# Rebuilding 64-bit weights as 32-bit numbers: two VectorE passes and two ScalarE passes in place of three and one

## The chip, the core and the metric

The kernel runs on one core of a Trainium2 chip. Its engines work side by side, each through its own queue in order: TensorE (PE, with its weight loads as PEld), VectorE (DVE), ScalarE (ACT), GpSimd (POOL) and SyncE (SP), which here issues DMA transfers. The metric is the device time of one execution, in microseconds. Three runs of the kernel before gave 382.01, 382.57 and 385.27 us; the median is 382.57 us.

## The reference

Three stages follow one another on inputs of 2 batches, 8 heads, 768 positions and 48 numbers per head.

```
state = 0
for t in range(768):                      # attention with a decay, per batch and head
    cur = outer(u * k[t], v[t])
    y[t] = r[t] @ (state + cur)
    state = w[t][:, None] * state + outer(k[t], v[t])
# first feed-forward block, x = y with heads side by side (384 wide)
xk = mu_k * x + (1 - mu_k) * x_prev ;  xr = mu_r * x + (1 - mu_r) * x_prev
k = relu(xk @ w_k) ;  v = (k * k) @ w_v ;  x = sigmoid(xr @ w_r) * v
# second block
h = gelu(x @ w_in) ;  u, v = halves of h
v_n = layer_norm(v) * g_ln ;  v_s = w_sg @ v_n + b_sg
out = x + (u * v_s) @ w_out
```

Five weight matrices (`w_k`, `w_v`, `w_r`, `w_in`, `w_out`) arrive as 64-bit floating-point numbers. The engines compute with 32 bits, so each is turned into 32-bit numbers on the chip.

## The kernel before, in words

**Units.** The attention is cut into groups of 384 positions (three chunks of 128; four groups) and pairs of heads (four), which makes 16 units, counted here from 1. For a unit, DVE makes running products of the decay (`pf`, `pr`) and scaled inputs (`rp`, `kp`; some on POOL), PE makes scores `sc`, DVE masks them (`am`), PE makes chunk states `kv`, ACT scales them (`pk`), DVE chains them (`us`, `ucar`), PE forms `y`, and DVE adds POOL's diagonal part `av` and writes `yt`. `av` comes from the unit's transfer `un`, multiplied twice on POOL (lines 360 and 361), summed on ACT (line 367) and multiplied again on POOL (line 372). PE then transposes `yt` to `xx`.

**Feed-forward steps.** For each group, `xx` is mixed with its neighbour position (`dx`, line 511), and multiplied by the weights (line 492). For most groups each operand is split in a high part (`...h`, a copy by ACT) and the rest (`...l`, a difference on DVE or POOL), and three products are added. For the first group the 32-bit weights `wk` and `wv` are used whole, and split afterwards: ACT copies `wkh`, `wvh` (line 241), POOL takes the difference `wkl`, `wvl` (line 242).

**Weights.** The 31 pieces of 128 x 384 weights (8 `wk`, 3 `wr`, 8 `wv`, 12 `wf`, the last for the second block) are converted by `load64` (lines 223 to 237). SP loads a piece as pairs of 32-bit words into a staging tile `stg`, of which there are three. ACT scales the high word by 2 to the power -112, which moves the exponent (line 233). DVE shifts left by 3 and clears the top bit (line 235), puts in the sign of the high word (line 236), and puts in the top three bits of the low word (line 237). The staging tile is free after line 237. The target tile of a `wf` piece comes from a ring of 24 tiles (tag `wl`), in which the first `wf` takes the place of a `wv` tile that POOL's line 242 reads.

**Order.** PE's order is written by hand, as a list of steps with planned times (`plan`). For the other engines each instruction gets a due time (`with at(...)`), and a scheduler at build time orders each engine's queue by due time and by its own estimate of when an instruction could start. SP and ACT also issue DMA transfers from their queues: SP the units' `ut` and the weights, ACT the units' `uv` and `un` (lines 211 and 213), so an instruction that waits at the head of such a queue also holds the transfers behind it.

Of the kernel before, what the change touches and what calls it, by code (L numbers as in the profile page):

```python
# [8 lines left out]
AF = mybir.ActivationFunctionType  # L9
ALU = mybir.AluOpType  # L10
# [47 lines left out]
def emit(tc, tin, nin, vt, consts, ubc, mu_k, mu_r, g_ln, b_sg, w_k, w_v, w_r, w_in, w_sgT, w_out, outT):  # L58
    nc = tc.nc
    V, A, PL, PE, SP = nc.vector, nc.scalar, nc.gpsimd, nc.tensor, nc.sync  # L60
# [162 lines left out]
    def load64(full, src, c0, c1, f0, f1, dl):  # L223
        n, f = c1 - c0, f1 - f0
        stg = pl["s"].tile([128, n, f, 2], U32, name="stg", tag="stg", bufs=B_STG)
        with at(dl - 7):
            SP.dma_start(
                stg.rearrange("p c f w -> p c (f w)"),
                src.bitcast(U32).rearrange("(c p) f -> p c f", p=128)[:, c0:c1, 2 * f0:2 * f1])
        wl, wh = stg[:, :, :, 0], stg[:, :, :, 1]  # L230
        bits = full.bitcast(U32)
        with at(dl - L_CV - 1):
            A.activation(full, wh.bitcast(F32), AF.Copy, scale=2.0 ** -112)
        with at(dl - L_CV):
            V.tensor_scalar(bits, bits, 3, 0x7FFFFFFF, ALU.logical_shift_left, ALU.bitwise_and)  # L235
            V.scalar_tensor_tensor(bits, wh, 0x80000000, bits, ALU.bitwise_and, ALU.bitwise_or)  # L236
            V.scalar_tensor_tensor(bits, wl, 29, bits, ALU.logical_shift_right, ALU.bitwise_or)  # L237

    def split_to(hi, lo, full, dl, e):
        with at(dl):  # L240
# [16 lines left out]
    def conv_moe1():  # L257
        def one(nm, i, src, box, dl):
            full1(nm, i, [128, KM, 128] if nm != "v" else [128, 1, DM])
            load64(wt[nm, i][0], src, *box, dl)  # L260
            if NAT[nm] == 0 or (nm == "v" and i >= NVN):
                split1(nm, i, dl - (3 if nm == "v" else 0))

        for f in range(KF):
            one("k", f, w_k, (0, KM, f * 128, f * 128 + 128), TS["k", 0, f])
        for f in range(KM):
            one("r", f, w_r, (0, KM, f * 128, f * 128 + 128), TS["r", 0, f])
        for f in range(KF):
            one("v", f, w_v, (f, f + 1, 0, DM), TS["v", 0, 0] + MM[0, "v"] * f)

    def conv_moe2():
        sp = split_ops[0]

        def make(key, shape):
            if sp:
                wt[key] = tuple(pl["b"].tile(shape, F32R, name="w2" + q, tag=f"w2{key[0]}{q}{key[1]}", bufs=1) for q in "hl")
            else:
                wt[key] = (pl["b"].tile(shape, F32, name="w2f", tag=f"w2{key[0]}f{key[1]}", bufs=1),)

        def fill(dst, src, box, dl):  # L280
            if sp:
                full = pl["w"].tile(list(dst[0].shape), F32, name="wf", tag="wl", bufs=NW1 + SPARE)
                load64(full, src, *box, dl)
                split_to(dst[0], dst[1], full, dl, PL)
            else:
                load64(dst[0], src, *box, dl)

        make(("in", "v"), [128, KM, DH])
        for x in range(KH):
            fill(part(wt["in", "v"], slice(None), slice(None), slice(x * 128, x * 128 + 128)), w_in,  # L290
                 (0, KM, DH + x * 128, DH + x * 128 + 128), TS["iv", 0, 0] - 6 + x)
        for x in range(KH):
            make(("in", x), [128, KM, 128])
            fill(wt["in", x], w_in, (0, KM, x * 128, x * 128 + 128), TS["iv", 0, 0] - 2 + x)
        for x in range(KH):
            make(("out", x), [128, 1, DM])
            fill(wt["out", x], w_out, (x, x + 1, 0, DM), TS["o", 0, 0] - 4 + x)
# [584 lines left out]
```

## Time and profile before

| | |
|---|---|
| runs | 382.01, 382.57, 385.27 us |
| profiled execution, first to last instruction | 380.1 us |
| busy: PE, PEld, DVE, ACT, POOL | 352.7, 317.3, 275.2, 183.6, 131.6 us |
| mean granted TensorE clock | 0.917 |

The profiled execution's own time is the span of 380.1 us; the median of the runs stands 2.5 us above it. All times inside the program are counted from the start of that span. A timeline row gives start, length, engine, line, operation and, in brackets, the idle time of the engine just before it and what ended it. PE counts as busy while a matmul is in its pipeline.

### The profile page before, as it was taken

Reading aid. Unit: us, or ns where it says so; the run is one execution under the profiler, and the core shown is the slowest. Engines: PE = TensorE matmul, PEld = TensorE weight load, DVE = VectorE, ACT = ScalarE, POOL = GpSimd, SP = SyncE. Lnnn points to the kernel's source line nnn. Section 1 sums busy time; section 2 is a strip of 40 time slices with the busy share of each in tenths; the row PEclk is TensorE's granted clock in tenths of the full one; section 3 lists DMA queues with packets and bytes.
Section 4 is the critical chain, followed back from the end, with each engine's and each line's share of the span. In section 5 each row is a group of like instructions: output and inputs, shape, how many; then the busy total and the mean of one; then the engine's idle time right before and its main releaser. Section 6 shows DMA issues by size and latency. Waiting matters only on the chain.

```text
span 380.1 us, 5744 instructions
## 1 busy us (share of the span) xinstructions
PE 352.7 (93%) x1971; PEld 317.3 (83%) x1971; DVE 275.2 (72%) x561; ACT 183.6 (48%) x542; POOL 131.6 (35%) x185
## 2 busy tenths in 40 slices
PE   5999898988897699899999999999999999999993
PEld 1889676657657598799989999989999998999993
DVE  6789988999977989963564997229898971735531
ACT  1354646866828576243565849456834323501100
POOL 0657974561699967541301653000000000000000
PEclk9555657989899699999999999999999999999999
DMA  7975357556641363400001130091233001010011
GB/s 176 273 238 177 98 186 222 152 160 211 206 127 31 111 187 101 128 5 2 0 2 42 43 113 13 0 280 26 63 84 80 10 3 62 2 62 0 2 65 69
DMA packets 27125, 36.20 MB, mean 95 GB/s; under 512 B 3312, under 2 KB 21584, under 8 KB 27088
## 3 DMA queue, kind: packets, MB, share of 16 engines
q1 hardware_dynamic: 23056, 29.57, 25.7%
q10 hardware_dynamic: 4032, 6.19, 5.4%
q8 instruction: 17, 0.28, 0.3%
q14 instruction: 20, 0.16, 0.1%
HBM read 33.39 MB, written 2.36 MB: 94 GB/s over the span
## 4 chain that ended last, share of the span: by engine, by line
PE 49%; DVE 10%; ACT 5%; issue 3%; POOL 3%; ACTq 0%; POOLq 0%
PE mm L492 22%; PE mn L492 22%; PE y L456 2%; DVE dx L511 2%; DVE wf L236 2%; DVE wf L237 1%; DVE kl L548 1%; POOL av L361 1%; PE sc L394 1%; ACT wvh L241 1%; ACT kr L547 1%; ACT kr L533 1%; ACT kh L546 1%; DVE xrl L515 1%; DVE wf L235 1%
## 5 line engine op out<-in xcount | busy, mean ns | idle before, releaser
L372 POOL TENSOR_TENSOR av<-uv,ac 128x96 f32<-128x96 f32 x48 | 30.5, 653 | 7.8 <-issue 4.4
L596 POOL TENSOR_SCALAR mv<-mv 128x1 f32<-128x1 f32 x12 | 2.9, 246 | 86.1 <-ACT vg L595 86.1
L456 PEld LDWEIGHTS y<-uv,am 128*128 128x128 f32 x192 | 29.2, 228 | 1.2 <-issue 0.6
L480 ACT ACTIVATE gah<-gt 128x384 fp32r<-128x384 f32 x16 | 8.4, 526 | 44.4 <-DVE gt L638 44.4
L533 ACT ACTIVATE kr<-mm 128x384 f32<-128x384 f32 x27 | 13.1, 485 | 30.9 <-PE mm L492 30.8
L456 PE MATMUL y<-uv,am 128*128 128x48 f32 x192 | 27.8, 303 | 0.0
L242 POOL TENSOR_TENSOR w2l<-wf,w2h 128x384 fp32r<-128x384 f32 x12 | 15.4, 1294 | 35.3 <-ACT w2h L241 35.0
L492 PE MATMUL mm<-xkh,wk 128*128 128x384 f32 x48 | 22.1, 609 | 0.0
L511 DVE SCALAR_TENSOR_TENSOR dx<-xx,par,dx 128x384 f32<-128x384 f32 x21 | 15.7, 760 | 8.4 <-ACT dx L508 8.3
L342 DVE TENSOR_TENSOR_SCAN pr<-ut,d1r 112x387 f32<-112x387 f32 x16 | 21.4, 1334 | 0.3
L367 ACT ACTIVATE av<-av 128x48 f32<-128x48 f32 x72 | 16.6, 245 | 10.0 <-POOL av L361 10.0
L394 PE MATMUL sc<-rp,kp 48*128 48x128 f32 x192 | 20.1, 352 | 1.3 <-DVE am L398 1.3
L492 PE MATMUL mm<-xkh,wkh 128*128 128x384 f32 x57 | 21.3, 373 | 0.0
L548 DVE TENSOR_TENSOR kl<-kr,kh 128x384 fp32r<-128x384 f32 x24 | 17.9, 747 | 4.2 <-ACT kr L547 4.0
L398 DVE TENSOR_TENSOR am<-sc,cst 128x384 f32<-128x384 f32 x32 | 17.0, 544 | 4.7 <-PE sc L394 4.7
L394 PEld LDWEIGHTS sc<-rp,kp 48*128 48x128 f32 x192 | 16.3, 243 | 4.7 <-issue 1.8
L492 PE MATMUL mn<-wsh,vh 128*128 128x384 f32 x60 | 20.1, 334 | 0.0
L492 PE MATMUL mn<-wsh,vl 128*128 128x384 f32 x60 | 20.1, 334 | 0.0
L492 PE MATMUL mn<-wsl,vh 128*128 128x384 f32 x60 | 20.1, 334 | 0.0
L492 PE MATMUL mm<-xkh,wkl 128*128 128x384 f32 x57 | 19.7, 346 | 0.0
L492 PE MATMUL mm<-xkl,wkh 128*128 128x384 f32 x57 | 19.7, 345 | 0.0
L338 DVE TENSOR_TENSOR_SCAN pf<-ut,d1f 112x387 f32<-112x387 f32 x16 | 15.6, 977 | 3.3 <-DMA ut<-tin 3.3
(209 smaller groups left out, 1153.2 us busy)
## 6 DMA issues: line engine op xcount, KB each, us to landing
ut<-tin SPq DMA_DIRECT2D x14, 505.8 KB, 4.2
un<-nin ACTq DMA_DIRECT2D x14, 288.0 KB, 3.8
stg<-w_k SPq DMA_DIRECT2D x8, 384.0 KB, 4.5
stg<-w_v SPq DMA_DIRECT2D x8, 384.0 KB, 3.6
stg<-w_in SPq DMA_DIRECT2D x8, 384.0 KB, 3.0
wq<-tin SPq DMA_DIRECT2D x16, 168.0 KB, 2.4
wsf<-w_sgT SPq DMA_DIRECT2D x12, 192.0 KB, 4.2
outT<-ot SPq DMA_DIRECT2D x12, 192.0 KB, 1.9
```

The costliest lines, as they stand in the source:

```text
L242: e.tensor_tensor(lo, full, hi.bitcast(F32), ALU.subtract)
L338: V.tensor_tensor_scan(pf[:, 0:n1], w[:, 0:n1], d1f[:, 0:n1], 1.0, ALU.mult, ALU.add)
L342: V.tensor_tensor_scan(pr[:, 1:wl][:, ::-1], w[:, 1:wl][:, ::-1], dr[:, 1:wl][:, ::-1], 0.0, ALU.mult, ALU.add)
L367: A.activation(z, z, AF.Copy, accum_out=ac[:, c, h:h + 1])
L372: PL.tensor_tensor(av[:, c].rearrange("p (h d) -> p h d", d=D), uv[i][:, c].rearrange("p (h d) -> p h d", d=D), ac[:, c, :, None].to_broad ...
L394: PE.matmul(sc[h][:, c], s["kp"][hs, c], s["rp"][hs, c], start=True, stop=True)
L398: V.tensor_tensor(am[:, h], sc[h], mask, ALU.mult)
L456: PE.matmul(o, l, r, start=(j == 0), stop=(j == len(mms) - 1), skip_group_check=True)
L492: PE.matmul(ps, l, r, start=(k == 0), stop=(k == len(prods) - 1))
L511: V.scalar_tensor_tensor(o, x[:, j, t0:t1], nu[:, j:j + 1], d, ALU.mult, ALU.add)
L533: A.activation(kr, ps, AF.Relu)
L548: V.tensor_tensor(kl, kr, kh.bitcast(F32), ALU.subtract)
```

## The change

`load64` gets a second ACT instruction and loses one of DVE's three. ACT reads the top byte of the low word (a byte in every eight), computes (byte + 0.5) / 32 - 0.5 and writes it, turned into a whole number, over the low word: that is the byte's three top bits. DVE then shifts the scaled high word left by 3 and puts in these bits in one pass, and puts in the sign in a second.

```
         with at(dl - L_CV - 1):
             A.activation(full, wh.bitcast(F32), AF.Copy, scale=2.0 ** -112)
+            top = stg.rearrange("p c f w -> p c (f w)").bitcast(mybir.dt.uint8).rearrange("p c (f w) -> p c f w", w=8)[:, :, :, 3]
+            A.activation(wl, top, AF.Copy, bias=0.5 / 32 - 0.5, scale=1.0 / 32)
         with at(dl - L_CV):
-            V.tensor_scalar(bits, bits, 3, 0x7FFFFFFF, ALU.logical_shift_left, ALU.bitwise_and)
+            V.scalar_tensor_tensor(bits, bits, 3, wl, ALU.logical_shift_left, ALU.bitwise_or)
             V.scalar_tensor_tensor(bits, wh, 0x80000000, bits, ALU.bitwise_and, ALU.bitwise_or)
-            V.scalar_tensor_tensor(bits, wl, 29, bits, ALU.logical_shift_right, ALU.bitwise_or)
```

In the changed kernel the second ACT instruction is line 235, the two DVE passes are lines 237 and 238, and all later lines count one more than before. PE's order is the same in both. The queues of ACT, DVE, POOL and SP are ordered anew at three places that the prediction speaks of.

First, ACT's queue where it issues the transfer of unit 10 (`un_980`). Before:

```order
L241 ACTIVATE wkh_779<-wk_115 128x384
L514 ACTIVATE xkh_1151<-dx_1158 128x384
L211 DMA uv_978<-nin 128x288
L559 ACTIVATE rs_1065<-mm_1055 128x384
L419 ACTIVATE pk_1071<-kv_1068,pb_867 112x48 x4
L233 ACTIVATE wv_239<-stg_240 128x384
L559 ACTIVATE rs_1088<-mm_1078 128x384
L213 DMA un_980<-nin 128x576
```

And now (`un_855` is the transfer of unit 9, which before stood further ahead):

```order
L560 ACTIVATE rs_1088<-mm_1078 128x384
L213 DMA un_855<-nin 128x576
L509 ACTIVATE dx_1153<-xx1_78,par_75 128x384
L509 ACTIVATE dx_1158<-xx1_78,par_75 128x384
...
L515 ACTIVATE xkh_1151<-dx_1153 128x384
L233 ACTIVATE wv_239<-stg_240 128x384
L235 ACTIVATE stg_240<-stg_240 128x384
L515 ACTIVATE xkh_1151<-dx_1158 128x384
L242 ACTIVATE wkh_779<-wk_115 128x384
L211 DMA uv_978<-nin 128x288
L213 DMA un_980<-nin 128x576
```

The steps on `dx` and `xkh` stood ahead of the transfer in both, but they now stand behind `rs_1088`; in DVE's queue the two `dx` now stand behind the `yt` of unit 8.

```order
L437 SCALAR_TENSOR_TENSOR us_1067<-ucar_81,pt_868,pk_1071 112x96
L237 SCALAR_TENSOR_TENSOR wv_218<-wv_218,stg_219 128x384
L437 SCALAR_TENSOR_TENSOR us_1067<-us_1067,pt_868,pk_1071 112x96
L238 SCALAR_TENSOR_TENSOR wv_218<-stg_219,wv_218 128x384
L460 TENSOR_TENSOR yt_726<-y_1090,av_871 128x3x96
L512 SCALAR_TENSOR_TENSOR dx_1153<-xx1_78,par1_76,dx_1153 128x384
L512 SCALAR_TENSOR_TENSOR dx_1158<-xx1_78,par1_76,dx_1158 128x384
```

That is DVE's queue of the changed kernel at the end of unit 8: the chain `us`, then `yt`, then the two `dx`.

Second, ACT's queue ahead of `pk_1286`, which unit 9's `y` needs. Before:

```order
L533 ACTIVATE kr_1240<-mm_1230 128x384
L386 ACTIVATE kt_1268<-kt_ps_1264 128x336
L546 ACTIVATE kh_1242<-kr_1240 128x384
L233 ACTIVATE wf_2299<-stg_2300 128x384
L547 ACTIVATE kr_1240<-kr_1240 128x384
L419 ACTIVATE pk_1286<-kv_1282,pb_992 112x48 x6
```

And now:

```order
L233 ACTIVATE wf_2299<-stg_2300 128x384
L235 ACTIVATE stg_2300<-stg_2300 128x384
L534 ACTIVATE kr_1240<-mm_1230 128x384
L387 ACTIVATE kt_1268<-kt_ps_1264 128x336
L547 ACTIVATE kh_1242<-kr_1240 128x384
L233 ACTIVATE wf_2308<-stg_2309 128x384
L548 ACTIVATE kr_1240<-kr_1240 128x384
L235 ACTIVATE stg_2309<-stg_2309 128x384
L420 ACTIVATE pk_1286<-kv_1282,pb_992 112x48 x6
```

The first `wf` has moved ahead of three steps, and a second `wf` with its extra step has come ahead of `pk_1286`.

Third, DVE's queue ahead of `us_1281`, the chain of unit 9. Before:

```order
L398 TENSOR_TENSOR am_1270<-sc_1272,cst_70 128x384
L235 TENSOR_SCALAR wf_2299<-wf_2299 128x384
L548 TENSOR_TENSOR kl_1243<-kr_1240,kh_1242 128x384
L236 SCALAR_TENSOR_TENSOR wf_2299<-stg_2300,wf_2299 128x384
L436 SCALAR_TENSOR_TENSOR us_1281<-pk_1286,pt_993 112x96
```

And now:

```order
L237 SCALAR_TENSOR_TENSOR wf_2299<-wf_2299,stg_2300 128x384
L238 SCALAR_TENSOR_TENSOR wf_2299<-stg_2300,wf_2299 128x384
L399 TENSOR_TENSOR am_1270<-sc_1271,cst_70 128x384
L399 TENSOR_TENSOR am_1270<-sc_1272,cst_70 128x384
L549 TENSOR_TENSOR kl_1243<-kr_1240,kh_1242 128x384
L237 SCALAR_TENSOR_TENSOR wf_2308<-wf_2308,stg_2309 128x384
L437 SCALAR_TENSOR_TENSOR us_1281<-pk_1286,pt_993 112x96
```

Both passes of the first `wf` and the first pass of the second now stand ahead of `us_1281`, and the two `am` behind the first `wf`. In POOL's queue one of the differences `wkl` has moved ahead of unit 10's `un` (lines 360 and 361); the rest of that stretch has the same instructions as before.

## Rows read from the trace of the kernel before

**Rows 1.** PE's waits by what ended them, from 40 to 110 us (ahead of the dots) and from 110 to 160 us (behind them): us in total, times, longest.

```profile
PE y L456 <- DVE us L436: 3.5, 5, 1.3
PE sc L394 <- DVE am L398: 1.3, 1, 1.3
PE mm L468 <- DVE yt L459: 1.0, 1, 1.0
PE mm L492 <- DVE wv L237: 1.0, 1, 1.0
...
PE y L456 <- DVE us L436: 3.7, 3, 2.9
PE y L456 <- ACT pk L419: 2.9, 1, 2.9
PE y L456 <- DVE pk L421: 1.6, 1, 1.6
PE kt_ps L468 <- DVE yt L459: 0.2, 1, 0.2
```

**Rows 2.** PE's waits from 160 us to the end.

```profile
PE kt_ps L468 <- DVE yt L459: 0.6, 1, 0.6
PE mn L492 <- DVE kl L548: 0.2, 1, 0.2
```

**Rows 3.** Stretches cut where the granted clock changes: stretch, then length, busy us (x instructions) of PE, PEld, DVE, ACT, POOL, then the granted clock, the DMA share and GB/s.

```profile
43.80:57.50 13.70, 13.00 (x51) 10.00 (x51) 12.18 (x24) 6.49 (x28) 11.32 (x14) 0.50 0.42 133
...
60.90:64.30 3.40, 3.40 (x6) 1.72 (x6) 2.69 (x7) 1.51 (x6) 1.46 (x3) 0.50 0.66 205
64.30:81.40 17.10, 15.48 (x87) 11.14 (x86) 16.71 (x33) 14.23 (x50) 9.59 (x14) 1.00 0.60 176
81.40:84.80 3.40, 3.40 (x9) 2.01 (x8) 3.40 (x7) 1.30 (x4) 2.40 (x3) 0.50 0.35 106
...
98.40:125.70 27.30, 22.57 (x101) 15.24 (x99) 22.04 (x31) 18.53 (x71) 26.87 (x28) 1.00 0.33 101
125.70:132.60 6.90, 4.91 (x20) 4.54 (x22) 6.87 (x9) 2.72 (x7) 6.41 (x8) 0.51 0.37 116
```

**Rows 4.** The pass that the change removes, and the near instructions for what it adds: groups by line with shapes; busy us, mean ns of one, then the idle time before them.

```profile
L235 DVE TENSOR_SCALAR wf<-wf 128x384 uint32<-128x384 uint32 x12 | 5.3, 446 | 2.0 <-ACT wf L233 2.0
L235 DVE TENSOR_SCALAR wk<-wk 128x384 uint32<-128x384 uint32 x8 | 3.8, 484 | 0.0
L235 DVE TENSOR_SCALAR wv<-wv 128x384 uint32<-128x384 uint32 x8 | 3.0, 370 | 1.1 <-ACT wv L233 1.1
L235 DVE TENSOR_SCALAR wr<-wr 128x384 uint32<-128x384 uint32 x3 | 1.7, 560 | 1.1 <-ACT wr L233 1.1
...
L236 DVE SCALAR_TENSOR_TENSOR wk<-stg,wk 128x384 uint32<-128x384 uint32 x8 | 4.9, 621 | 0.0
...
L233 ACT ACTIVATE wk<-stg 128x384 f32<-128x384 f32 x8 | 4.5, 564 | 0.0
...
L533 ACT ACTIVATE kr<-mm 128x384 f32<-128x384 f32 x27 | 13.1, 485 | 30.9 <-PE mm L492 30.8
L508 ACT ACTIVATE dx<-xx,par 128x384 f32<-128x384 f32 x24 | 13.9, 610 | 0.8 <-DVE xrl L515 0.7
L511 DVE SCALAR_TENSOR_TENSOR dx<-xx,par,dx 128x384 f32<-128x384 f32 x21 | 15.7, 760 | 8.4 <-ACT dx L508 8.3
```

**Rows 5.** The chain that ended last, in order of time, around unit 9's `y`: start us, us, what.

```profile
121.95 1.01 POOL wvl L242
...
122.98 0.56 ACT wf L233
...
125.39 1.27 DVE wf L236
126.66 0.98 DVE us L436
...
127.69 0.74 PE y L456 x2
```

**Rows 6.** POOL's timeline ahead of that.

```profile
98.75 0.83 POOL L360 TENSOR_TENSOR av<-un,u_sb 128x288 f32<-128x288 f32 x1 [2.85 <-DMA un<-nin]
...
100.41 2.59 POOL L242 TENSOR_TENSOR wkl<-wk,wkh 128x384 fp32r<-128x384 f32 x2
...
118.41 9.11 POOL L242 TENSOR_TENSOR wvl<-wv,wvh 128x384 fp32r<-128x384 f32 x8
```

**Rows 7.** The issue of unit 10's `un` on ACT (second row) with the step that held ACT (first row), and the last matmul of unit 8's `y`.

```profile
93.22 0.55 ACT L233 ACTIVATE wv<-stg 128x384 f32<-128x384 f32 x1 [1.25 <-DMA stg<-w_v]
93.22 0.33 ACTq L213 DMA_DIRECT2D un<-nin  x1
...
94.44 0.46 PE L456 MATMUL y<-us,rp 112*128 112x96 f32 x2 [0.83 <-DVE us L436]
```

**Rows 8.** From issue to landing of the transfers `un` (first) and `stg` (second).

```profile
DMA to landing us min/median/max: 2.5/4.1/5.8
...
DMA to landing us min/median/max: 2.7/3.6/7.1
```

**Rows 9.** ACT and DVE just ahead of unit 9's `y`.

```profile
121.40 0.47 ACT L533 ACTIVATE kr<-mm 128x384 f32<-128x384 f32 x1
...
123.85 0.28 ACT L419 ACTIVATE pk<-kv,pb 112x48 f32<-112x48 f32 x1
...
120.56 1.00 DVE L398 TENSOR_TENSOR am<-sc,cst 128x384 f32<-128x384 f32 x2
```

**Rows 10.** DVE's removed pass where it ran within POOL's stretch from 98.75 to 122.96 us, and POOL's difference in that stretch (times one: minimum, median, maximum ns).

```profile
99.27 0.53 DVE L235 TENSOR_SCALAR wv<-wv 128x384 uint32<-128x384 uint32 x1 [0.35 <-ACT wv L233]
...
L242 POOL TENSOR_TENSOR wvl<-wv,wvh x8: 998/1212/1343, 118.4 to 126.2; 128x384 fp32r<-128x384 f32 x8
```

## The prediction

> **What bounds the kernel now.** I began with PE's waits, because PE is busy for 352.7 of the 380.1 us. From 160 us to the end it waits 0.8 us in all [rows 2], though 12 of the 31 pieces of weights are partly converted there: nothing can be won in that half, and little lost while PE stays fed. From 40 to 110 us it waits 6.8 us, each time for DVE (3.5 for `us`, 1.3 for `am`, 1.0 for `yt`, 1.0 for a `wv`), and from 110 to 160 us 8.4 us [rows 1]. Two single waits of 2.9 us make most of the latter; both belong to unit 9's `y`. Next the stretches by granted clock: after several of these waits PE is granted 0.50, its lower level of 1.2 GHz, for 3.4 us at a time, and 6.9 us after the two long ones [rows 3]. DVE is busy nearly without a break there, 16.71 of 17.10 us from 64.30 to 81.40 [rows 3]. So DVE does hold PE back, by many small waits, up to 104 us.
>
> The chain of waits then shows what holds unit 9's `y` [rows 5]: a POOL difference `wvl` ends at 122.96; it frees the tile that ACT's first `wf` needs; ACT does `wf` at 122.98, and `pk`, next but one behind it in ACT's queue, starts at 123.85 [rows 9]; DVE's `us` ends at 127.64 and PE goes on at 127.69. POOL in turn works without idle time from 98.75, when the transfer `un` of unit 10 has landed, to the end of its eight `wvl` at 127.52, that is 118.41 + 9.11 [rows 6]. **PE's arrival does not set this time; POOL's start does.** Whatever PE gains ahead of 104 us it must wait for again here, unless `un` lands earlier.
>
> **The change part by part.**
>
> *Removed:* 31 DVE passes, 5.3 + 3.8 + 3.0 + 1.7 = 13.8 us of busy time, 0.35 to 0.56 us each [rows 4]. The 19 of `wk`, `wr` and `wv` (8.5 us) lie ahead of 104 us, where PE waits 6.8 us. I expect most of these waits to shrink. Their worth at the end is nothing by itself, for the reason just given; without that cover they would be worth up to 6.8 us and half of the low-clock stretches among them (60.90 to 64.30 and 81.40 to 84.80, so 3.4 us).
>
> *Added:* 31 ACT instructions. The trace has none that reads single bytes eight apart; the nearest rows are the step beside it, 0.56 us, and, as bounds, 0.49 and 0.61 us for other steps of this size [rows 4]. I take 0.56: 17 us more on an engine that is busy 48% of the span. ACT has room on average, so the price lies in what stands behind them in its queue.
>
> *The two DVE passes that stay* read and write as the old ones did, so their price (0.62 us, 1.27 beside POOL) is unchanged [rows 4, 5]. The staging tile is free after the same last pass, so SP's loads keep their rule.
>
> *Moved, first place: the transfer of unit 10.* In the new ACT queue `un_980` stands behind two `xkh`, one `wkh` and the pairs of three `wv` pieces, and the `xkh` need the two `dx`, which now stand behind unit 8's `yt` on DVE. When does unit 8's `y` end? Before, at 94.44 + 0.46 = 94.90 [rows 7]. With none of the 5.8 us of waits ahead of it and no low-clock stretch it would be 94.90 - 5.8 - 3.4 = 85.7. I take 91, in the middle and a little late, because ACT's `pk` for it now has a `wv` pair between its halves that waits for a staging load. From there: the piece `wv_239` takes the staging tile of `wv_218`, whose last pass ends just ahead of `yt`, so at about 91; its load lands 3.6 us later [rows 8]; the pair, `xkh` and `wkh` are four ACT steps of 0.56 us: 91 + 3.6 + 2.2 = 96.8, where before it was issued at 93.22 [rows 7]. (By DVE's side it is sooner: `yt` and two `dx` of 0.76 us.) It lands 4.1 us later by the median, 5.5 by the one before (98.75 - 93.22); I take 4.6 [rows 6 to 8]: 101.4.
>
> *POOL's stretch* from there to the `wvl` in question was 122.96 - 98.75 = 24.2 us; one `wkl` of 1.3 us (half of 2.59) now stands ahead of it, so 22.9 us [rows 5, 6]. It ends at 101.4 + 22.9 = 124.3: **1.3 us later than before**. The ends of this term: with `y` at 85.7 the same steps give 118.6, 4.4 us earlier; with `y` at 94.90 and the median landing, 127.7, 4.7 us later.
>
> *Does the pass that is gone make POOL faster?* Only one such pass ran within that stretch, 0.53 us long, while the `wvl` took from 0.998 to 1.343 us each [rows 10]; POOL's time hangs on other DVE work. The Trainium skill (SBUF — State Buffer, section Who interferes with whom, with the reading of the diagram ahead of it) says that a DVE pass in a two-port mode and one with two SBUF inputs both shut POOL out for their whole length. By that rule the removed pass would give back at most its 0.53 us and the sum would be 384.2; but the passes that stay have two inputs and shut POOL out as well. The trace agrees so far that DVE's passes take 1.27 us beside POOL and 0.62 on the mean.
>
> *Moved, second and third place: ahead of `pk` and `us` of unit 9.* Before, five ACT steps from 121.40 to 123.85 took 2.1 us without the wait for POOL, so 0.42 each back to back [rows 9]. Now eight stand between the `wvl` and `pk`: wf, extra, kr, kt, kh, wf, square, extra, 3.4 us instead of 0.9. On DVE, from the end of the `wvl`: 1.0 until the extra step is done, two passes of 1.27 beside POOL (busy until 4.6), `am` twice 1.0 [rows 9], `kl` and the second wf's first pass at 0.62, `us` 0.98: 6.7 us, where before it was 127.64 - 122.96 = 4.7. That is 2.0 later; with every pass at 0.62 and `us` at 0.4 it is 0.2 later. I take **1.5 later**, nearer to the upper end, since POOL runs on. All of PE's later work stands behind this.
>
> *After 128 us* the waits are 0.9 + 1.6 + 0.2 = 2.7 us [rows 1]. DVE has finished one piece more by then and saves a pass on the rest; the chains there run through POOL too. I take 0.8 us off (ends 0 and 2.7). The low clock from 125.70 to 132.60 I leave as it is (one stretch of 3.4 us more or less: 1.7 us either way). *From 160 us on:* DVE loses 7 passes, ACT gets 4 or so; PE waits 0.8 us in all: nothing.
>
> **Sum:** +1.3 + 1.5 - 0.8 = +2.0 us on the profiled execution's 380.1 us, so a span of 382.1. The median of the runs stands 2.5 us above that span; on it, 382.6 + 2.0 = **384.6 us**. Ends: -4.4 + 0.2 - 2.7 - 1.7 = -8.6 and +4.7 + 2.0 + 1.7 = +8.4.
>
> **The rivals.**
>
> *The relief arrives* (faster). DVE's small waits go, unit 8's `y` ends near 88 and `un` lands by 98; POOL's `wvl` ends 2.1 us earlier, the new order costs 0.5 because POOL is out of DVE's way sooner, 2 us of the later waits go, and one low-clock stretch: -2.1 + 0.5 - 2.0 - 1.7 = -5.3, 377.3 us. For it: DVE full up to 104 us and all waits there on DVE. Against it: the queue order above, which puts `un` behind more.
>
> *ACT's queue waits for staging loads* (slower). The extra step stands at the head of ACT's queue until its load lands; ACT's step already waited 1.25 us for one ahead of `un` [rows 7], and now a second reader per piece is placed by due time, at times before the first. `pk`, `kr` and `un` wait behind it. It decides from the point where `un` is issued after about 98.5 instead of 96.8: +3.1 there, +2.0 for the order, +0.4 of clock: +5.5, 388 us. For it: three staging tiles and loads of 2.7 to 7.1 us [rows 8].
>
> *Nothing reaches the end:* the two terms at the hold-up cancel, 382.6 us.
>
> *The extra step costs more than it seems:* reading bytes at 1.1 us each instead of 0.56 would put 17 us more on ACT, and two of them (1.1 us) plus a later `un` (2 to 3 us) on the path: 388 us too. Nothing in the trace shows such a step.
>
> **How the numbers follow.** Forecast 0.37, the relief 0.20, staging loads 0.23, nothing 0.15, the dear step 0.05. About 1% (3.8 us) is what a measurement of this kernel can tell from no change. Faster by over 1%, below 378.7: most of the relief, 0.16. Slower by over 1%, above 386.4: the slower two and a little of the forecast, 0.31. Within 1%: 0.53. The range from 378.0 to 389.5 leaves out the outer part of the relief and of the slow cases, some 0.2. The forecast's own range is 382.6 to 386.5.
>
> **What would show it.** Right, if: DVE's busy time falls by about 14 us and ACT's rises by about 17; PE's waits ahead of 104 us are fewer than 6.8 us, yet it waits longer than 5.7 us at unit 9's `y`; POOL's `un` multiplication comes at 100 to 103 us; `pk` follows the freeing `wvl` by over 3 us; PE waits nearly nothing after 160 us. Wrong, if that multiplication starts before 98 us, if ACT idles for `stg` more than a few us, if the byte step takes far from 0.56 us, or if PE's waits after 160 us exceed 2 us.

## The result and the profile after

The changed kernel takes 387.48 us (median; 384.79 to 389.81), the kernel before, run beside it, 382.87 us (381.05 to 386.64): a ratio of 1.0104 with a 95% interval of 1.0077 to 1.0131, so slower by some 4.6 us. The profiled execution spans 384.9 us, 4.8 more than before. The forecast was 384.6 us.

The conversion itself got cheaper, as the page's busy times and the groups by line with shapes (busy us, mean ns of one, idle time before) show:

```profile
PE 349.8 (91%) x1971; PEld 313.9 (82%) x1971; DVE 265.2 (69%) x530; ACT 197.4 (51%) x573; POOL 126.6 (33%) x185
```

```profile
L235 ACT ACTIVATE stg<-stg 128x384 uint32<-128x384 uint8 x31 | 17.0, 550 | 3.8 <-DMA stg<-w_r 1.7 <-DMA stg<-w_v 1.5 <-DMA stg<-w_in 0.6
...
L237 DVE SCALAR_TENSOR_TENSOR wk<-wk,stg 128x384 uint32<-128x384 uint32 x8 | 5.8, 726 | 0.0
...
L238 DVE SCALAR_TENSOR_TENSOR wk<-stg,wk 128x384 uint32<-128x384 uint32 x8 | 4.8, 601 | 0.0
```

The byte step takes 0.55 us, the step beside it 0.56 [rows 4]. By the page's totals DVE is busy 10.0 us less than before and ACT 13.8 more. The groups say 13.5 less (59.5 to 46.0 us for the conversion on DVE) and 17.0 more: steps that follow each other closely overlap in the trace by some 0.1 us, and the totals count that time once. PE itself is busy 2.9 us less, so the lost time is waiting. PE's waits, from 40 to 110, from 110 to 160 and from 160 us to the end:

```profile
PE kt_ps L469 <- ACT kt L387: 8.1, 2, 7.2
PE y L457 <- DVE us L437: 6.3, 6, 1.9
PE mm L469 <- DVE yt L460: 0.9, 1, 0.9
PE kt_ps L384 <- ACT kt L387: 0.7, 1, 0.7
...
PE y L457 <- DVE us L437: 2.5, 2, 2.2
PE y L457 <- ACT pk L420: 0.7, 1, 0.7
...
PE y L457 <- DVE pk L422: 1.7, 1, 1.7
PE kt_ps L469 <- DVE yt L460: 1.6, 2, 1.0
PE mn L493 <- DVE kl L549: 0.6, 1, 0.6
PE y L457 <- DVE us L437: 0.2, 1, 0.2
```

Against [rows 1, 2] the first stretch waits 16.0 us instead of 6.8, the second 3.2 instead of 8.4, the last 4.1 instead of 0.8. The new one is 7.2 us for ACT's `kt`, behind unit 8; PE stopped at 97.4. ACT's timeline tells what `kt` stood behind, and where unit 10's `un` was issued:

```profile
97.48 0.49 ACT L560 ACTIVATE rs<-mm 128x384 f32<-128x384 f32 x1 [1.91 <-PE mm L493]
97.87 0.54 ACT L233 ACTIVATE wv<-stg 128x384 f32<-128x384 f32 x1
...
98.33 0.78 ACTq L213 DMA_DIRECT2D un<-nin  x1
...
100.45 0.51 ACT L242 ACTIVATE wkh<-wk 128x384 fp32r<-128x384 f32 x1
103.27 0.55 ACT L233 ACTIVATE wv<-stg 128x384 f32<-128x384 f32 x1 [2.31 <-DMA stg<-w_v]
103.72 0.54 ACT L235 ACTIVATE stg<-stg 128x384 uint32<-128x384 uint8 x1
104.16 0.43 ACT L387 ACTIVATE kt<-kt_ps 128x336 f32<-128x336 f32 x1
```

Of the 7.2 us the staging load is 2.31: a `wv` step waited for it at the head of the queue, and `kt` with it. The rest is the steps that stand ahead, which ran back to back from 97.48 to 100.96 and again from 103.27. The load was late. SP's timeline, of the kernel before and then of the changed one, has the loads of the eight `wv` pieces:

```profile
68.16 0.35 SPq L227 DMA_DIRECT2D stg<-w_v  x1
...
73.95 11.84 SPq L227 DMA_DIRECT2D stg<-w_v  x4
...
89.53 3.73 SPq L227 DMA_DIRECT2D stg<-w_v  x3
```

```profile
69.52 0.35 SPq L227 DMA_DIRECT2D stg<-w_v  x1
...
83.13 11.48 SPq L227 DMA_DIRECT2D stg<-w_v  x5
...
98.73 2.02 SPq L227 DMA_DIRECT2D stg<-w_v  x2
```

The second `wv` load goes out at 83.13 instead of 73.95, because until then all three staging tiles were held. In ACT's new queue the byte steps of `wr_182`, `wr_193` and `wv_204` (`stg_183`, `stg_194`, `stg_205`) stand early and ran at 69.07, 71.42 and 73.49 us, but the scaling steps of these pieces, without which DVE's passes on them do not begin, stand far behind and ran at 79.33, 83.93 and 88.52. The first of the three tiles came free with a DVE pass that ended at 83.07. From the list of ACT's queue in the changed kernel:

```
L235 ACTIVATE stg_183<-stg_183 128x384
L542 ACTIVATE kh_907<-kr_905 128x384
L235 ACTIVATE stg_194<-stg_194 128x384
L213 DMA un_742<-nin 128x576
L235 ACTIVATE stg_205<-stg_205 128x384
...
L242 ACTIVATE wrh_179<-wr_171 128x384
L387 ACTIVATE kt_917<-kt_ps_913 128x336
L233 ACTIVATE wr_182<-stg_183 128x384
```

Finally the hold-up at unit 9's `y`, from POOL's, ACT's, DVE's and PE's timelines (to be held against [rows 5, 6]):

```profile
103.68 0.80 POOL L361 TENSOR_TENSOR av<-un,u_sb 128x288 f32<-128x288 f32 x1 [1.53 <-DMA un<-nin]
...
113.58 0.79 POOL L361 TENSOR_TENSOR av<-un,u_sb 128x288 f32<-128x288 f32 x1 [0.39 <-DMA un<-nin]
...
121.10 9.33 POOL L243 TENSOR_TENSOR wvl<-wv,wvh 128x384 fp32r<-128x384 f32 x8
```

```profile
109.36 0.52 ACT L515 ACTIVATE xkh<-dx 128x384 fp32r<-128x384 f32 x1 [1.32 <-DVE dx L512]
...
109.75 0.45 ACTq L213 DMA_DIRECT2D un<-nin  x1
...
125.97 0.56 ACT L233 ACTIVATE wf<-stg 128x384 f32<-128x384 f32 x1 [0.93 <-POOL wvl L243]
...
129.29 1.24 ACT L420 ACTIVATE pk<-kv,pb 112x48 f32<-112x48 f32 x6
```

```profile
132.15 0.30 DVE L437 SCALAR_TENSOR_TENSOR us<-pk,pt 112x96 f32<-112x96 f32 x1
```

```profile
132.50 0.60 PE L457 MATMUL y<-us,rp 112*128 112x96 f32 x2 [2.23 <-DVE us L437]
```

Unit 10's `un` (first row) is multiplied 4.9 us later than before, the `wvl` that frees the tile of `wf` ends 3.0 later, `us` ends 4.8 later (132.45 against 127.64), and the program ends 4.8 later. POOL does not work through from the first row to the third: it pauses 1.7 us between them, the last time at 113.58 for unit 11's `un`, which ACT issued at 109.75 behind an `xkh` that waited for DVE's `dx`. From there POOL runs without a pause to the end of its eight `wvl`.

### The profile page after: what moved, and what is told of

Same layout as the page of the kernel before. It is cut to its first block, busy times and chain, and to the rows that moved or that the text cites. A ratio compares the mean times of both kernels' runs of the same rounds, so it can differ in the third digit from the quotient of the medians.

```text
span 384.9 us, 5748 instructions
## 1 busy us (share of the span) xinstructions
PE 349.8 (91%) x1971; PEld 313.9 (82%) x1971; DVE 265.2 (69%) x530; ACT 197.4 (51%) x573; POOL 126.6 (33%) x185
## 5 line engine op out<-in xcount | busy, mean ns | idle before, releaser
L373 POOL TENSOR_TENSOR av<-uv,ac 128x96 f32<-128x96 f32 x48 | 25.6, 549 | 11.7 <-issue 4.8
L457 PEld LDWEIGHTS y<-uv,am 128*128 128x128 f32 x192 | 28.0, 220 | 1.0
L457 PE MATMUL y<-uv,am 128*128 128x48 f32 x192 | 26.8, 296 | 0.0
L512 DVE SCALAR_TENSOR_TENSOR dx<-xx,par,dx 128x384 f32<-128x384 f32 x21 | 17.7, 864 | 13.1 <-ACT dx L509 13.1
L534 ACT ACTIVATE kr<-mm 128x384 f32<-128x384 f32 x27 | 13.2, 488 | 23.7 <-PE mm L493 22.3
L493 PE MATMUL mm<-xkh,wk 128*128 128x384 f32 x48 | 20.7, 577 | 0.0
L339 DVE TENSOR_TENSOR_SCAN pf<-ut,d1f 112x387 f32<-112x387 f32 x16 | 16.7, 1043 | 4.9 <-DMA ut<-tin 4.9
L457 PE MATMUL y<-us,rp 112*128 112x96 f32 x48 | 11.1, 337 | 9.6 <-DVE us L437 9.5
L362 POOL TENSOR_TENSOR av<-av,un 128x288 f32<-128x288 f32 x16 | 18.6, 1166 | 1.1
```

What stands on the lines that cost most here:

```text
L339: V.tensor_tensor_scan(pf[:, 0:n1], w[:, 0:n1], d1f[:, 0:n1], 1.0, ALU.mult, ALU.add)
L362: PL.tensor_tensor(av, av, n[:, 1], ALU.mult)
L373: PL.tensor_tensor(av[:, c].rearrange("p (h d) -> p h d", d=D), uv[i][:, c].rearrange("p (h d) -> p h d", d=D), ac[:, c, :, None].to_broad ...
L457: PE.matmul(o, l, r, start=(j == 0), stop=(j == len(mms) - 1), skip_group_check=True)
L493: PE.matmul(ps, l, r, start=(k == 0), stop=(k == len(prods) - 1))
L512: V.scalar_tensor_tensor(o, x[:, j, t0:t1], nu[:, j:j + 1], d, ALU.mult, ALU.add)
```

## The experiments

**Is it the work or the order?** The first two kernels fix the queues of ACT, DVE, POOL and SP with order-only edges, from a list of each instruction's place:

```
+    for eng, order in ORDER.items():
+        ins = [i for i in nc.cur_bb.bb.instructions if str(i.engine).endswith("." + eng) ...]
+        for a, b in zip(order, order[1:]):
+            tc.add_manual_dep(ins[b], ins[a].name, ...)   # b is issued behind a
```

> The changed conversion (extra ACT step, two DVE passes), but the queues of ACT, DVE, POOL and SP hold the order of the kernel before: the extra step stands right behind its scaling step, the two passes at the places of the old second and third. Nothing is left out. Theory A (the time was lost by the new order of the queues): the loss is gone, 379 to 383 us, PE's wait of 7.2 us for `kt` near 100 us is gone, and unit 10's `un` is multiplied on POOL before 100 us. Theory B (the work itself costs: 17 us more on ACT, passes that read two tiles beside POOL): 386 to 389 us, as the changed kernel.

> The conversion of the kernel before (one ACT step, three DVE passes), but the four queues hold the order of the changed kernel. Nothing is left out. Theory A (order): 386 to 391 us, PE waits 5 us or more for `kt` near 100 us, unit 10's `un` is multiplied at 102 us or later. Theory B (work): 381 to 384 us.

Measured: 377.68 us, ratio 0.9857 (0.977 to 0.9945), and 397.41 us, ratio 1.0346 (1.0263 to 1.0429). The order costs, the work gains: with the old order the changed conversion is faster than both kernels, with the new order the old conversion is slower than both. Both lie outside the ranges of Theory A, on its side: it had 379 to 383 us for the first and 386 to 391 for the second. Each kernel ran four times, and the profile of the first is its fastest execution, 3.4 us under the median. In the first, unit 8's `y` and unit 10's `un` come 5.6 and 6.1 us earlier than before (PE's and POOL's timelines):

```profile
88.17 1.17 PE L515 MATMUL y<-us,rp 112*128 112x96 f32 x4 [1.97 <-DVE us L495]
...
122.15 0.74 PE L515 MATMUL y<-us,rp 112*128 112x96 f32 x2 [2.02 <-DVE us L495]
```

```profile
92.69 1.22 POOL L419 TENSOR_TENSOR av<-un,u_sb 128x288 f32<-128x288 f32 x1 [2.35 <-DMA un<-nin]
```

In the second the long wait for `kt` is back, and unit 9's `y` is 8.4 us later than before (PE's timeline):

```profile
105.43 0.90 PE L526 MATMUL kt_ps<-cst,yt 128*128 128x128 f32 x3 [6.88 <-ACT kt L444]
...
136.09 0.74 PE L514 MATMUL y<-us,rp 112*128 112x96 f32 x2 [3.61 <-DVE us L494]
```

**Is the hold-up at unit 9 what ends the program?** The steps of three `wf` pieces are put behind unit 9's `pk` and `us`:

```
-        with at(dl - L_CV - 1):
+        with at(dl - L_CV - 1), after(late, 0):     # tc.issue_after(unit 9's last pk) if late
...
-        with at(dl - L_CV):
+        with at(dl - L_CV), after(late, 1):         # tc.issue_after(unit 9's second us) if late
```

> The kernel before, with ACT's and DVE's steps of the first three `wf` pieces put behind unit 9's `pk` and `us` in their queues. Theory A with the hold-up as predicted (POOL's `wvl` holds `wf`, and `wf` holds `pk` and `us`): the two waits of PE of 2.9 us each at unit 9's `y` shrink to under 1 us each and the end comes 3 to 6 us earlier, 377 to 380 us. Rival C (PE is held there by `am` or by POOL's diagonal part in any case, or the later `wf` are missed afterwards): 382 to 384 us.

> The changed kernel with the same steps of the first three `wf` pieces put behind unit 9's `pk` and `us`. Theory A: PE's waits at unit 9's `y`, 2.9 us in all, go; the wait of 7.2 us for `kt` stays; 384 to 385.5 us against 387.5. Rival C: no change, 387 to 389 us. If the hold-up were the whole loss, 382 us or less.

Measured: 383.17 us for the kernel before, ratio 0.9985 (0.9951 to 1.0019): no gain; 383.10 us for the changed one, 1.0007 (0.9967 to 1.0046): 4.4 us of the changed kernel's loss are gone. On the kernel before Theory A missed. Unit 9's `y` does come 3.3 us earlier, but PE then waits again at the next unit, and its `y` is only 1.6 us earlier (136.85 before). PE's and DVE's timelines:

```profile
122.64 0.46 PE L465 MATMUL y<-pk,rp 112*128 112x96 f32 x2 [1.50 <-ACT pk L424]
...
124.37 0.46 PE L465 MATMUL y<-us,rp 112*128 112x96 f32 x2 [1.27 <-DVE us L443]
...
135.24 0.46 PE L465 MATMUL y<-us,rp 112*128 112x96 f32 x2 [2.19 <-DVE us L443]
```

```profile
127.14 2.10 DVE L242 SCALAR_TENSOR_TENSOR wf<-stg,wf 128x384 uint32<-128x384 uint32 x1
...
134.90 0.29 DVE L443 SCALAR_TENSOR_TENSOR us<-pk,pt 112x96 f32<-112x96 f32 x1
```

DVE has no pause from 122.24 to this `us`. Unit 10's last `pk` is ready at 133.16; seven passes on the postponed `wf` pieces, 6.8 us, stand on DVE between the `us` of unit 9 and that of unit 10. So the postponed work took back half of the gain one unit later.

On the changed kernel the gain is larger than expected: 2.6 us at unit 9's `y` (129.90), the rest behind 160 us, where PE waits 1.3 us (0.7 and 0.6) instead of 4.1. `un` is still multiplied late there (104.71), the last `wv` load still goes out at 100.51 and PE still waits 8.7 us for a `kt`. So nearly all of the loss reaches PE through the steps of the `wf` pieces that stand ahead of unit 9's `pk` and `us`.

**Which late step counts, `kt` or `un`?** The changed kernel's own order is kept, but for one or two moves:

```
 ACT:  ... rs_1088  un_855  dx  dx ... xkh  wkh  uv_978  un_980  wv_246  stg_247  kt_1042
 kt_ahead:  kt_1042 stands ahead of rs_1088
 un_ahead:  un_980 stands right behind un_855; on POOL wkl_778 behind un_980's multiplications
```

> The changed kernel with its own queue orders, but ACT's step `kt` that PE waited 7.2 us for stands five pairs of `wv` steps earlier, ahead of `rs_1088`, so that no staging load stands ahead of it. Nothing is left out. Theory A (POOL's stretch from unit 10's `un` sets unit 9's `y`, so PE's wait for `kt` is covered): the wait of 7.2 us goes, PE waits so much longer at unit 9's `y`, and the time stays at 386 to 389 us. Rival D (the wait for `kt` is the loss): 380 to 382 us.

> The changed kernel with its own queue orders, but unit 10's `un` is issued right behind unit 9's on ACT, and POOL does its two multiplications ahead of the first `wkl`. Nothing is left out. Theory A: `un` is multiplied at 97 to 99 us instead of 103.7, POOL's stretch ends 4 to 6 us earlier, and unit 9's `y` comes as early as PE arrives there, 2.9 us earlier: 384 to 385.5 us. Rival D: no change, 386.5 to 389 us.

> Both moves in one. Theory A: neither limit is left at its place, unit 9's `y` comes at 126 to 127.5 us instead of 132.5: 380.5 to 383 us, more than the two gains alone. Rival D: as with `kt` alone, 380 to 382 us, and then `kt` alone must have given it too.

Measured: 387.10 us (1.0108; 1.0045 to 1.017), 388.76 us (1.0147; 1.0104 to 1.019) and 387.09 us (1.01; 1.0062 to 1.0137). None of the moves gains. With `kt` ahead PE's wait of 7.2 us is gone; waits of 4.7 us for `wv` come in part in its place, and unit 9's `y` is 0.9 us earlier (131.62). The time stays, as Theory A said: that wait was covered. With `un` ahead the time is what Rival D had said, no gain (386.5 to 389 us), but its cause, `kt`, is ruled out by the run with `kt` ahead. The run with both moves misses both theories. In it `un` is multiplied at 96.75, 6.9 us earlier, and yet POOL's eight `wvl` begin at 120.16 instead of 121.10. POOL's timeline has the reason:

```profile
96.75 1.11 POOL L419 TENSOR_TENSOR av<-un,u_sb 128x288 f32<-128x288 f32 x1
...
100.19 1.42 POOL L301 TENSOR_TENSOR wkl<-wk,wkh 128x384 fp32r<-128x384 f32 x1 [1.26 <-ACT wkh L300]
104.21 1.42 POOL L301 TENSOR_TENSOR wkl<-wk,wkh 128x384 fp32r<-128x384 f32 x1 [2.59 <-ACT wkh L300]
...
108.67 0.50 POOL L431 TENSOR_TENSOR av<-uv,ac 128x96 f32<-128x96 f32 x1 [1.80 <-ACT av L426]
...
112.64 0.79 POOL L419 TENSOR_TENSOR av<-un,u_sb 128x288 f32<-128x288 f32 x1 [0.96 <-DMA un<-nin]
```

POOL now waits 1.26 + 2.59 + 1.80 + 0.96 = 6.6 us for ACT: for `wkh`, for its sums, for unit 11's `un`. In ACT's queue the second of these `wkh` stands behind the last two `wv` pieces, which wait for their loads; the sums and unit 11's `un` stand behind it. What sets the start of the `wvl` is the last of these waits: from the multiplication of unit 11's `un` it is 7.5 us, without a pause, with both moves (112.64 to 120.16) as in the changed kernel (113.58 to 121.10). That `un` was issued at 108.28, behind an `xkh` that waited 1.71 us for DVE's `dx`.

**What turned the order?**

> The changed kernel without the extra ACT step: two DVE passes, a shift with a mask of one tile and the sign; the three lowest bits of each weight are left out. The scheduler sets the order. Theory A (the extra ACT step is what turns the order): unit 10's `un` stands early in ACT's queue as before, 375 to 380 us. Theory E (fewer DVE passes turn the order): 385 us or more.

Measured: 383.85 us, 1.0008 (0.9972 to 1.0044). Both theories miss on the time. The loss does not come without the byte step, but the gain doesn't either: the scheduler's order for two passes multiplies unit 10's `un` at 99.00 (98.75 before), and unit 9's `y`, at 126.18, is 1.5 us earlier; the end is not. Of the 5.9 us that the changed conversion gained in the old order, nothing arrives here: a pass less on DVE did not shorten the program in this order.

**Why the scaling steps stood late.** The low half of a split `wr` took a tile of the ring `wl`, as the pieces do. My reading was that the ring hands out its tiles in the order in which the program names them, so that `wr_182` had to be placed behind the low half of `wr_171`, and so behind its split. Two kernels give the low halves a ring of their own:

```
 SPARE = 5
+NWL = NW1 + SPARE - KM
...
-        lo = pl["w"].tile(shape, F32R, name="w" + nm + "l", tag="wl", bufs=NW1 + SPARE)
+        own = nm == "r"
+        lo = pl["w"].tile(shape, F32R, name="w" + nm + "l", tag="wrl" if own else "wl", bufs=KM if own else NWL)
```

> The changed kernel, but the low halves of the split `wr` have a ring of three tiles of their own, and the ring `wl` has three fewer; so the scaling step of the next `wr` piece need not be placed behind the split of the one before it. The scheduler sets the order; nothing is left out. Theory F (the scaling steps of two `wr` and one `wv` piece, placed late, hold all three staging tiles, SP's loads of `wv` start 9 us late, and ACT's queue then waits on them): the first of the five loads is issued near 74 us instead of 83, the wait for `kt` is gone, unit 10's `un` is multiplied at 96 to 100 us, 379 to 383.5 us. Rival G (the other turns in ACT's queue carry the loss): 385.5 to 389 us.

> The kernel before with the same rings. Theory F: there was no such knot, 381 to 384 us. Rival G: no different, 381 to 384 us; it is the control.

Measured: 382.68 us (0.9981; 0.9951 to 1.0011) and 382.23 us (0.9984; 0.9945 to 1.0024). The changed kernel's loss is gone, as Theory F said, and the pairs stand together again (each byte step 1 to 7 places from its scaling step), so the ring is what tore them. The loads of `wv` are out by 91.50 us instead of 100.75 (SP's timeline):

```profile
71.60 6.01 SPq L228 DMA_DIRECT2D stg<-w_v  x3
81.18 0.33 SPq L198 DMA_DIRECT2D ut<-tin  x1
81.61 9.89 SPq L228 DMA_DIRECT2D stg<-w_v  x5
```

But two of its signs miss. PE still waits 6.03 us for a `kt`, now one unit earlier, and `un` is multiplied at 104.66, not at 96 to 100 us. What came right is the other end of the hold-up: here only one `wf` piece stands ahead of `pk` and `us`, and `us` ends 129.89 - 125.34 = 4.6 us after that `wf` starts, where the changed kernel took 6.5. ACT's and DVE's timelines:

```profile
125.34 0.55 ACT L234 ACTIVATE wf<-stg 128x384 f32<-128x384 f32 x1 [0.76 <-POOL wvl L244]
```

```profile
106.45 1.00 DVE L341 TENSOR_TENSOR_SCAN pf<-ut,d1f 112x387 f32<-112x387 f32 x1 [5.48 <-DMA ut<-tin]
...
128.84 1.05 DVE L439 SCALAR_TENSOR_TENSOR us<-pk,pt 112x96 f32<-112x96 f32 x1
```

So Theory F's chain is not shown by its time. The loads come 9.3 us earlier here, but unit 11's `un` is issued at 109.84, no earlier than in the changed kernel (109.75), and the eight `wvl` begin at 120.79 instead of 121.10. POOL's last wait is for a `wkh` (2.83 us, to 110.41). Ahead of both, on ACT, stands again the `xkh` that waits for DVE's `dx`, here 5.41 us; DVE in turn waited 5.48 us (first row) for a `ut`, which SP issued only at 102.52. Of the 2.6 us gained at unit 9's `y` (129.95), 1.9 come from the piece less ahead of `pk` and `us`, and 0.6 from POOL.

**Shortening POOL's stretch.** On top of these rings the eight `wvl` go to DVE:

```
-        split_to(hi, lo, full, dl, PL)
+        split_to(hi, lo, full, dl, V if nm == "v" else PL)
```

> The changed kernel with the rings of the run wr_own_ring, and the eight differences `wvl` on DVE instead of POOL. Theory A (POOL's stretch, 9.3 us of which are `wvl`, sets unit 9's `y`, and DVE is idle for some 9 us ahead of it): unit 9's `y` comes when PE arrives, 374 to 379 us. Rival H (the eight passes stand ahead of `am` and `us` on DVE and hold them): 381 to 385 us.

> The kernel before with the rings and with `wvl` on DVE. Theory A: also faster, but less, as DVE has 13 us more to do ahead of it: 377 to 381 us. Rival H: 382 to 386 us.

Measured: 379.56 us (0.9892; 0.9834 to 0.9949) and 379.25 us (0.9875; 0.9814 to 0.9937). Beside the kernels with these rings alone both gain some 3 us, and with it the change is worth nothing. The first lies between the ranges of Theory A and Rival H, the second in that of Theory A. But unit 9's `y`, at 129.02 and 126.50, is 0.9 us earlier than with the rings alone in the changed kernel (129.95) and 1.3 later in the kernel before (125.24), and in the former PE still waits 5.0 us for `pk` there. Both profiles are the slowest of four executions. So the gain is measured, but that it comes by way of unit 9's `y`, as Theory A has it, is not shown.

## Why the prediction came out as it did

The time lies in the stated range and on the forecast side, but outside the forecast's own range (382.6 to 386.5) by 1 us. The end of the chain that it named, from the `wvl` by `wf` to `pk` and `us`, is what the loss passes through; how the chain starts it had wrong, and two signs that it had named for being wrong came true, so the number owes something to the width of the range. The stages of the chain, in us (start of the multiplication of unit 10's `un` and of unit 11's, start of the first `wf`, pieces of `wf` on ACT ahead of unit 9's `pk`, end of `us`, span), each from one profiled execution:

| | `un` 10 | `un` 11 | `wf` | pieces | `us` | span |
|---|---|---|---|---|---|---|
| before | 98.75 | 109.27 | 122.98 | 1 | 127.64 | 380.1 |
| forecast | 101.4 | | 124.3 | 2 | 130.4 | 382.1 |
| changed | 103.68 | 113.58 | 125.97 | 2 | 132.45 | 384.9 |
| old order, new work | 92.69 | 103.88 | 117.56 | 1 | 122.10 | 372.4 |
| new order, old work | 104.32 | 116.65 | 129.06 | 2 | 136.04 | 395.7 |
| changed, `wf` late | 104.71 | 113.47 | 128.09 | 0 | 129.13 | 380.4 |
| both ahead | 96.75 | 112.64 | 125.05 | 2 | 131.52 | 385.1 |
| own ring | 104.66 | 112.94 | 125.34 | 1 | 129.89 | 380.4 |

- *Removed and added:* right. The conversion on DVE went from 59.5 to 46.0 us (sums of its groups), and the passes that stay from 45.7 to 46.0. The byte step took 0.55 us against 0.56 taken.
- *First place, unit 10's `un`:* the sign right, the size not: POOL's stretch ended 3.0 us later instead of 1.3. Two steps failed. "I take 91" for the end of unit 8's `y`: it was 94.5, 0.4 earlier than before, since PE's waits for `us` ahead of it grew from 3.5 to 6.3 us. And the issue at 96.8: it came at 98.33, behind `rs`, for which ACT waited 1.91 us for PE. The landing took 5.3 us against 4.6 taken. The stretch on POOL was 125.97 - 103.68 = 22.3 us against 22.9 taken, pauses of 1.7 us included.
- *POOL's speed:* no gain came from the pass that is gone. The eight `wvl` took 9.33 us, 9.11 before [rows 6]. By the removed pass's 0.53 us the sum would have been 384.1, not 384.2. The Trainium skill (SBUF — State Buffer, section Who interferes with whom) says that a DVE pass with two SBUF inputs contends with a POOL instruction that reads SBUF, and that the one that starts first holds the other up for its whole length. The trace agrees so far that the two such passes on a `wf` beside the `wvl` took 1.23 and 1.24 us, and one behind them 0.55.
- *"POOL's start does":* this failed where it takes that start to be unit 10's `un`. POOL did not work without idle time from there, as the stretch assumes. With both moves that `un` is multiplied 6.9 us earlier than in the changed kernel, and POOL's stretch ends 0.9 earlier. In every kernel with the changed order, and in the one with own rings, the eight `wvl` begin some 7.5 to 7.9 us after the multiplication of unit 11's `un`, without a pause on POOL in between. POOL's last wait before is for that `un` (for a `wkh` with own rings), and in the three kernels followed here it stood in ACT's queue behind the same `xkh`, which waits for DVE's `dx`. In the changed kernel this `dx` (108.63) stands right behind DVE's passes on the last two `wv` pieces, so the late loads are in its chain; in the run with own rings, with the loads 9.3 us earlier, it comes at 108.78 for another reason. What the late loads cost by themselves no run shows.
- *Second and third place, ahead of `pk` and `us`:* right. 6.5 us instead of 4.7, so 1.8 later, against 1.5 taken; the run with own rings, where one piece less stands there, has 4.6. With the steps of these pieces put behind `pk` and `us` 4.4 of the 4.6 us are gone.
- *After 128 us:* wrong. I took 0.8 us off; from the end of `us` to the end of the program it is 252.5 us in both kernels. "PE waits nearly nothing after 160 us" failed with 4.1 us.
- *Not foreseen:* the wait of 7.2 us for `kt`, and that pairs of ACT steps would be torn apart. That wait cost nothing by itself, as the run with `kt` ahead shows.
- *The signs:* two came, the byte step's price and `pk` over 3 us behind the freeing `wvl` (3.4). The busy times moved by 10.0 and 13.8 us, not 14 and 17. PE's waits ahead of 104 us did not become fewer, its waits at unit 9's `y` were 2.9 us instead of over 5.7, and `un` came later than 100 to 103. Of the signs of being wrong, ACT idled 7.7 us for `stg` (4.7 before), and PE waited over 2 us after 160.

The sum of the terms was +1.3 + 1.5 - 0.8; measured are +3.0, +1.8 and 0. That is nearly the sum of the rival in which ACT's queue waits for staging loads (+3.1, +2.0, +0.4; 388 us), and 0.23 was low for it beside 0.37. Its mechanism was at work in part: ACT did wait for late loads, but `un` was issued at 98.33, just under its dividing line of 98.5, and was held there by `rs` and not by a load. The relief (377.3 us forecast; unit 8's `y` near 88, `un` by 98) is what the change gives in the old order: 377.68 us, with 88.2 to 89.3 and 92.7. The point against it, the queue order, decided.

In the run of the old work in the new order, 259.7 us pass from the end of `us` to the end, 7.2 more than in the two kernels compared. PE waits 1.8 us more after 160 us (5.9 against 4.1), and after such waits it is granted 0.50 for two more stretches, 166.5 to 169.9 and 251.9 to 258.7, in which it is busy 9.4 us. Matmuls of 128x384 follow each other every 0.32 us there and every 0.17 at the higher level, so these stretches cost an estimated 4.4 us.

What stays open: what the late staging loads cost by themselves, since the runs that moved them or moved `un` met another wait there, at the `xkh` ahead of unit 11's `un`; and where the 3 us come from that the `wvl` on DVE gain. A kernel with the byte step and all three DVE passes in an order of the scheduler's own wasn't tried.

## What to carry to other kernels

Where a scheduler orders the queues at build time, a change has two effects, its work and the order it brings about; fixing the old order around the new work, and the reverse, tells them apart in two runs, and here they have opposite signs: -5.9 us and +13.8 us against the kernel before. When two steps on one engine are needed for one staging tile, see to it that they stay together and that no ring's order puts one behind unrelated work: here tiles held between them made the later loads up to 9.2 us late, though no run shows what that alone cost. Work that is not needed yet should not stand ahead of what the busiest engine waits for: moving it behind gave back 4.4 of the 4.6 us here. And where several late steps meet at one place, moving one of them alone can gain nothing, because the engine then waits for the next.

## What the runs showed of the hardware

An ACT step that reads single bytes eight apart and writes words eight bytes apart costs no more than one on 32-bit numbers: 550 ns mean over 31, against 546 to 565 ns for the scaling step.

In two places here a transfer in ACT's queue was issued before a step ahead of it had run. `un` was issued at 98.33, while the last step that stands ahead of it in the queue, `wkh`, started at 100.45; in the kernel before it went out at 93.22, the moment the step at the head got its load [rows 7]. So in these two places waits ahead of it held it, and run times did not. I had added four step times of 0.56 us there.

PE's clock fell at 91.7, within a wait of 1.91 us for `us` that ended at 92.27, and PE was granted 0.50, its lower level of 1.2 GHz, for 17.0 us, during which it was busy 8.5 us; before, the low stretch there lasted 3.4 us. These are two of the stretches of the changed kernel (length, busy us of PE, PEld, DVE, ACT, POOL, granted clock, DMA share, GB/s):

```profile
9.70:33.90 24.20, 23.65 (x124) 20.51 (x124) 20.48 (x37) 10.18 (x59) 15.82 (x28) 0.51 0.73 207
...
91.70:108.70 17.00, 8.47 (x22) 6.18 (x23) 15.45 (x25) 11.88 (x35) 9.54 (x11) 0.50 0.70 225
```

The first low stretch ended at 33.9 instead of 40.4 us, so the sum over the program is about the same: 30.7 + 13.7 + 6.8 + 3.4 + 6.9 = 61.5 us before, 24.2 + 14.3 + 3.1 + 17.0 + 3.8 = 62.4 after, with PE busy 58.3 and 52.2 us in them. It does not explain 4.8 us.
